# Talking-heads attention and a squared-ReLU network on one core: the first batch's first 22 score chunks taken through four 32-column tiles and one mixing matmul instead of six full matmuls

## The chip, the core and the metric

The kernel runs on one core of one Trainium2 chip. The metric is device time in microseconds, the median of several runs. One more execution was recorded by the hardware profiler; all durations below come from that one. The engines are TensorE (PE in the profile, its weight loads PEld), VectorE (DVE), ScalarE (ACT), GpSimd (POOL) and SyncE (SP).

## The reference, cut to what is computed

```python
# batch 8, 12 heads, 448 positions, head size 64; w_pre and w_post are 12x12
scores = (q @ k^T) / 8                        # per head
scores = einsum('bhij,hg->bgij', scores, w_pre)   # heads mixed before the softmax
attn   = softmax(scores, axis=-1)
attn   = einsum('bhij,hg->bgij', attn, w_post)    # and after it
x      = (attn @ v), heads side by side       # 3584 x 768
out    = relu(x @ w_in)**2 @ w_out            # 768 -> 2048 -> 768
```

## The kernel before, in words

Work is cut by batch. In each batch the 448 query rows are taken in chunks of 10 (`CH`), 45 of them: 10 rows times 12 heads give 120 partitions, so that one matmul with a small constant matrix can mix the heads of a chunk. A unit of work goes through these stages:

- **T** (`emit_T`): q and k of a batch are transposed on TensorE and copied out of PSUM into `qkt` (`tev` tasks). In batch 0 head pairs arrive in three groups `a`, each as a q and a k load.
- **QK** (`emit_QK`): scores of a tile of queries, copied out into `stage` (24 copies of 448 columns for 12 heads of two tiles in batch 0). DMAs from SP (`emit_rel`) move the rows of a chunk from `stage` into a slot of `dring`, which brings all heads of a row together.
- **pre** (`emit_pre`): one 64-wide matmul pair per half chunk mixes the heads with `wk1`. The result is in PSUM.
- **exp** (`after_pre`): ScalarE takes the exponential into `pring` with row sums; `rec` and `fold` put 1/sum into the post-mixing matrix `wk2s` (on VectorE for the first five pairs of chunks, on GpSimd after that).
- **post** (`emit_post`): mixes the heads again and transposes; two copies per pair of chunks into `a2t`.
- **AV**, **F1** (`relu`, `sq`) and **F2** (`oev`, `odma`): attention times v, and the two layers of the network.

Batch 0 has no finished `stage` at the start, so its first 22 chunks (`ND`) take another way in `emit_direct`: VectorE multiplies q with the scaled `w_pre` into `qs` (`emit_scale`, tasks `sc`, which hold 12 mixed copies of each query row), and for each chunk six full 128x128 matmuls, one per head pair, add up the already mixed scores in one PSUM bank (L922). exp reads that bank. `qs` lies in the space of `w_out_sb` (16 chunks) and `h2t` (6 chunks), so `w_out` is loaded after the chunks in its space are done.

TensorE's order is not found at run time: `ORDER` is a string of stream numbers (0 T, 1 QK, 2 pre, 3 post, 4 AV, 5 direct, 6 and 7 F1, 8 and 9 F2), and `_Plan.run` takes the next unit of that stream. The copies out of PSUM are `FLEX` tasks, which the planner gives to ACT or DVE; each engine's list is then fixed. PSUM has 8 banks of 512 columns; a QK or post unit takes two, a chunk of `emit_direct` one. Where the planner sees a gap ahead of a unit in the first 60 us it puts matmuls on constant data there (`warm`).

TensorE works in several tilings, and the planner charges a change of tiling: full 128x128 ("full": direct, F1 of two batches), 64x128 ("row": some QK, post, F1, F2), 64x64 ("quad": T, some QK, pre, F1, F2) and 128x64 ("cols": AV).

## Time and the profile before

| what | us |
|---|---|
| median of 3 runs (lowest, highest) | 519.81 (518.43, 520.98) |
| span of the profiled execution | 520.6 |
| TensorE busy | 505.5 |
| ScalarE busy | 425.6 |
| VectorE busy | 398.7 |
| GpSimd busy | 203.4 |
| first F2 matmul on the chain of work that ended last | 90.46 |

The profiled execution is given by its span, from the first instruction to the last; no separate run time stands beside it, and its span lies 0.8 us above the median of the runs. Matmuls are pipelined: one of 448 columns is shown as about 354 ns, while a row of them starts every 190 ns or so. So TensorE's cost is read from the chain of work (start, length, how many), not from the mean of one matmul. "Busy" of an engine in a stretch counts overlapping instructions once, and the sum of ACT and DVE over twice the stretch says how dense the two engines that empty PSUM are.

### The profile page before, as it was taken

The page shows a single profiled execution, that of the slowest core. Times are in us where ns is not written, and L with a number is a line of the kernel's source. Part 1 is how long each engine was busy: PE and PEld are TensorE (multiplying, and loading weights), DVE is VectorE, ACT ScalarE, POOL GpSimd, SP SyncE. Part 2 cuts the span into 40 slices and gives each one's busy share as a digit, 9 for nine tenths or more (in the row PEclk, how much of TensorE's full clock was granted, in tenths as well). Part 3 has the DMA queues.
Part 4 walks back from the last instruction along what each step waited for, and adds up shares of the span by engine and source line. Part 5 has one row for each costly group of instructions (what it writes and reads, how often), then busy time and mean ns, then how long its engine had stood idle before and what let it go on. Part 6 is the DMA issues. An engine that isn't in the chain of part 4 may idle for free.

```text
span 520.6 us, 25670 instructions
## 1 busy us (share of the span) xinstructions
PE 505.5 (97%) x10859; PEld 340.1 (65%) x10859; DVE 398.7 (77%) x1004; ACT 425.6 (82%) x1206; POOL 203.4 (39%) x404
## 2 busy tenths in 40 slices
PE   8999999899999999999999999999999999999996
PEld 4555777668766665667657665667666666678963
DVE  6967988789987869967997779976887669757430
ACT  4799999879998898989887999988788879878311
POOL 9914364325632384134622464225440333123010
PEclk9999999999999999999999999999999999999999
DMA  8999999646893699347974689457972568432013
GB/s 160 208 218 184 197 194 184 156 107 144 167 180 86 136 177 197 92 112 166 178 156 90 153 175 179 98 111 170 167 151 59 125 140 148 91 81 69 4 39 90
DMA packets 82724, 72.12 MB, mean 139 GB/s; under 512 B 13578, under 2 KB 80090, under 8 KB 82602
## 3 DMA queue, kind: packets, MB, share of 16 engines
q0 software_dynamic: 36944, 32.81, 38.5%
q1 hardware_dynamic: 45370, 37.38, 29.7%
q8 instruction: 89, 1.46, 1.1%
q14 instruction: 33, 0.27, 0.1%
q10 hardware_dynamic: 288, 0.20, 0.1%
HBM read 45.70 MB, written 11.01 MB: 109 GB/s over the span
## 4 chain that ended last, share of the span: by engine, by line
PE 92%; DMA 3%; DVE 2%; issue 2%; ACT 1%; POOL 0%; DVEq 0%
PE ps L1413 17%; PE ps L1278 12%; PE ps L1427 9%; PE ps L1292 9%; PE ps L1133 8%; PE ps L1052 8%; PE ps L1257 6%; PE ps L1211 6%; PE ps L922 5%; PE ps L974 4%; DMA dring<-stage 3%; PE ps L825 2%; PE ps L1362 2%; PE ps L986 2%; PE ps L649 1%
## 5 line engine op out<-in xcount | busy, mean ns | idle before, releaser
L1070 ACT ACTIVATE pring<-ps 128x448 bf16<-128x448 f32 x360 | 192.0, 550 | 12.6 <-PE ps L1052 7.3
L1101 POOL TENSOR_TENSOR wk2s<-wk2b,rinv 128x120 bf16<-128x120 bf16 (+1 forms) x179 | 69.0, 389 | 223.5 <-DVE rinv L1094 222.8
L527 DVE CAST a2t<-ps 128x480 bf16<-128x480 f32 (+1 forms) x201 | 122.1, 640 | 18.4 <-PE ps L1133 16.9
L527 DVE CAST stage<-ps 128x448 bf16<-128x448 f32 (+1 forms) x189 | 112.8, 618 | 19.0 <-PE ps L986 8.7
L526 ACT ACTIVATE stage<-ps 128x448 bf16<-128x448 f32 (+1 forms) x171 | 87.9, 549 | 18.2 <-PE ps L986 10.6
L526 ACT ACTIVATE a2t<-ps 128x480 bf16<-128x480 f32 x167 | 88.2, 570 | 15.5 <-PE ps L1133 15.0
L1413 PE MATMUL ps<-w_out_sb,h2t 64*128 64x384 bf16 x1056 | 95.9, 322 | 0.0
L1070 ACT ACTIVATION_READ_ACCUMULATOR pring<-ps 128x1 f32 x360 | 76.9, 214 | 0.0
L1133 PEld LDWEIGHTS ps<-wk2s,pring 60*128 60x128 bf16 x2880 | 54.9, 93 | 24.7 <-issue 5.8
L1278 PE MATMUL ps<-xt,w_in_sb 64*128 64x448 bf16 (+2 forms) x840 | 70.6, 309 | 0.0
L1413 PEld LDWEIGHTS ps<-w_out_sb,h2t 64*128 64x128 bf16 x1056 | 48.4, 94 | 31.1 <-PE ps L1052 0.7
L1459 POOL DMA_DIRECT2D out_dram<-osb x59 | 36.9, 632 | 75.9 <-DVE osb L527 25.8
L1133 PE MATMUL ps<-wk2s,pring 60*128 60x60 bf16 x2880 | 62.3, 187 | 1.9 <-issue 1.4
L1052 PE MATMUL ps<-dring,wk 64*64 64x448 bf16 (+1 forms) x676 | 61.5, 359 | 2.4 <-issue 1.2
L1427 PE MATMUL ps<-w_out_sb,h2t 64*64 64x384 bf16 x1216 | 57.4, 323 | 0.9 <-issue 0.8
L1323 DVE TENSOR_SCALAR h1t<-ps 128x448 bf16<-128x448 f32 (+2 forms) x96 | 46.2, 488 | 12.6 <-PE ps L1278 9.1
L1292 PE MATMUL ps<-xt,w_in_sb 64*64 64x448 bf16 (+1 forms) x1008 | 54.5, 345 | 0.8 <-issue 0.6
L1332 DVE TENSOR_TENSOR h2t<-h1t 128x448 bf16<-128x448 bf16 (+2 forms) x176 | 52.0, 331 | 1.4 <-ACT h1t L1322 0.9
L1322 ACT ACTIVATE h1t<-ps 128x448 bf16<-128x448 f32 (+2 forms) x80 | 35.4, 448 | 19.7 <-PE ps L1278 13.9
L1094 DVE RECIPROCAL rinv<-rowsum 128x2 f32<-128x2 f32 (+1 forms) x184 | 29.3, 160 | 28.2 <-ACT pring L1070 27.1
L1278 PEld LDWEIGHTS ps<-xt,w_in_sb 64*128 64x128 bf16 x840 | 38.3, 94 | 18.1 <-DVE rinv L1094 0.5
L1427 PEld LDWEIGHTS ps<-w_out_sb,h2t 64*64 64x64 bf16 x1216 | 38.2, 107 | 13.8 <-issue 2.0
(70 smaller groups left out, 595.0 us busy)
## 6 DMA issues: line engine op xcount, KB each, us to landing
dring<-stage SPq DMA_DIRECT2D x309, 105.0 KB
out_dram<-osb POOLq DMA_DIRECT2D x45, 192.0 KB, 3.7
qraw<-in_q_dram POOLq DMA_DIRECT2D x42, 112.0 KB, 5.3
kraw<-in_k_dram POOLq DMA_DIRECT2D x42, 112.0 KB, 6.2
w_in_sb<-in_moe_w_in_dram POOLq DMA_DIRECT2D x8, 384.0 KB, 16.3
w_out_sb<-in_moe_w_out_dram POOLq DMA_DIRECT2D x8, 384.0 KB, 11.9
vraw<-in_v_dram POOLq DMA_DIRECT2D x21, 128.0 KB, 4.8
vraw<-in_v_dram POOLq DMA_DIRECT2D x21, 96.0 KB, 5.0
```

Source lines behind the costliest of these rows:

```text
L526: return eng.activation(o, i_, AF.Copy)
L527: return eng.tensor_copy(o, i_)
L1052: r_ = eng.matmul(ps[64 * y:64 * y + 64, gr.banks[x], 0:S], wk1[64 * x:64 * x + 64 - R0 * x, :], dring[64 * x:64 * x + 64 - R0 * x, (g0 + ...
L1070: return eng.activation(pring[:, pr, 0:S], ps[:, gr.banks[x], 0:S], AF.Exp, accum_out=rowsum[:, rs, :])
L1101: return eng.tensor_tensor(wk2s[:, p0:p0 + n, :], i0.to_broadcast([128, n, PR]), rinv[:, p0:p0 + n, :].to_broadcast([128, n, PR]), ALU.mult)
L1133: r_ = eng.matmul(ps[:, gr.banks[x], o0:o0 + PR], pring[64 * x:64 * x + PR, pr + y, j0:j0 + 2 * PJ], wk2s[64 * x:64 * x + PR, pr + y, :], ...
L1278: r_ = eng.matmul(ps[:, g.banks[x], 0:n], w_in_sb[64 * y:64 * y + 64, ft, t * 128:(t + 1) * 128], xt[64 * y:64 * y + 64, ft, c0:c1], start ...
L1292: r_ = eng.matmul(ps[64 * z:64 * z + 64, g.banks[x], 0:n], w_in_sb[64 * y:64 * y + 64, ft, t:t + 64], xt[64 * y:64 * y + 64, ft, c0:c1], s ...
L1323: return eng.tensor_scalar(h1t[:, box[0], 0:n], ps[:, g.banks[x], 0:n], 0.0, None, op0=ALU.max)
L1332: return eng.tensor_tensor(h2t[:, t16, o0:o0 + n], h1t[:, box[0], 0:n], h1t[:, box[0], 0:n], ALU.mult)
L1413: r_ = eng.matmul(ps[:, g.banks[hh], 0:FH], h2t[64 * y:64 * y + 64, t16, col:col + 128], w_out_sb[64 * y:64 * y + 64, t16, hh * FH:(hh + 1 ...
L1427: r_ = eng.matmul(ps[64 * z:64 * z + 64, g.banks[hh], 0:FH], h2t[64 * y:64 * y + 64, t16, col + 64 * z:col + 64 * z + 64], w_out_sb[64 * y ...
```

## The change

For each of the 22 chunks the scores of the 12 heads are now first computed unmixed, 10 rows of each head, and laid out on 120 of 128 partitions, then mixed by one matmul. The stationary operand for that is `qs[rows, chunk, j, part, 0:32]`, zero but for the columns that belong to one head, so that a matmul of 128 rows (two heads) and 32 columns puts two or one heads' rows in their places. Four such tiles `j` lie side by side in the 128 columns of TensorE, and two matmuls per tile (`part` 0 and 1) add up: 8 matmuls per chunk. Then VectorE or ScalarE copies the 448 columns into a ring of 8 slots (`sring`, task `sv`), and one full matmul with `wks` (scaled `w_pre` with a mask) gives the mixed scores.

- Gone: 132 full matmuls (L922), 36 VectorE multiplications `sc` (L900), four small ones for `wq` (L613), six of the twelve copies of q and k of batch 0 into `qkt` (for q), the load `wall`.
- New: 176 matmuls of 32 columns (L932 of the kernel after), 22 full matmuls `mx` (L949), 22 copies `sv` of 448 columns (14 on ACT and 8 on DVE), 12 copies of 64x220 into `qs` (10 on DVE, 2 on ACT), three copies of the rest of q for QK (128x2x228), a zero fill of `qs` of 2816 32-bit columns on ACT instead of one of 768 and one of 288, a sum for a mask and two products for `wks`, and eight small loads of `w_pre` on SP instead of one. The matmuls of a chunk need all six head pairs of q and k; before, two pairs were enough to begin.
- `w_out` is loaded after all 22 chunks, not after 16. `ORDER` and the unit sizes in `EVENTS` are new throughout, so all units of the kernel stand in a new order. Matmuls of other kinds are the same in number; three more `warm` matmuls stand in it (20 for 17).
- Counted along TensorE's order, the tiling changes 252 times before and 267 times now; ahead of the first F2 matmul 82 and 116 times, and after it 170 and 151 times. Up to that matmul both orders hold the same units, but for one pre unit (90 matmuls before, 86 now) and two QK units in another tiling.

The core of the diff (`ORDER` is left out but for a line):

```diff
-    "0001501510105151555555555555555551335510015555555553335510021551355553255310055511255321"
+    "00101001101155555a15aa5155a555aa30aa3011a55aa1a53351553aaa555a0a33aa5a0a2a33323001144114"
...
+        def fn_wreps(eng, en):
+            for j in range(TL):
+                for c, n, h in ((0, 2, head(j, 0)), (2, 1, head(TL + j // 2, j % 2))):
+                    src = bass.AP(w_pre.tensor, h * H, [[2 * H, n], [0, CH], [1, H]])
+                    r0 = 32 * j + c * CH
+                    eng.dma_start(wreps[r0:r0 + n * CH, :], src).then_inc(sem_ws.handle, 16)
...
-                            emit_scale(p)
+                                for x in range(2):
+                                    rows = slice(64 * x, 64 * x + 64)
+                                    j, part, o0 = (p, 0, x * CH) if p < TL else (
+                                        2 * (p - TL) + x, 1, 2 * CH)
+                                    r_ = copy(eng, en, qs[rows, :, j, part, o0:o0 + CH],
+                                              ps_bf[rows, g.banks[0], u * S:u * S + ND * CH].rearrange(
+                                                  "p (c a) -> p c a", a=CH))
...
-                for p in ps_:
-                    r_ = eng.matmul(ps[:, g.banks[0], 0:S],
-                                    qs[:, p, y:y + 2, :].rearrange("p i g -> p (i g)"),
-                                    qkt[:, 0, p, 1, :],
...
+                for part in range(2):
+                    for j in range(TL):
+                        p = TL + j // 2 if part else j
+                        r_ = eng.matmul(ps[32 * j:32 * j + 32, g.banks[0], 0:S],
+                                        qs[:, c, j, part, :], qkt[:, 0, p, 1, :],
+                                        start=(part == 0), stop=(part == 1))
...
+            t_sv = add("sv%d" % c, FLEX, fn_sv, [t, dir_done.get(c - NSR)], c_ev(S), -500.0 + c)
+            g.readers[0].append(t_sv)
+            g2 = _Group(1)
+
+            def fn_mx(eng, en):
+                return eng.matmul(ps[:, g2.banks[0], 0:S], wks[:, :], sring[:, slot, :],
+                                  start=True, stop=True)
...
-                emit_load_w(1, [dir_done[c] for c in range(NDW)])
+                emit_load_w(1, [dir_done[c] for c in range(ND)])
```

Three places show how it moves instructions. The first is TensorE from the last transpose of batch 0 on. Before, the six-matmul chunks are L922 (`ps<-qkt,w_out_sb`), QK is L974 and L986, post is L1133:

```order
L821 MATMUL ps<-ident,kraw 64x2x32 x28
L922 MATMUL ps<-qkt,w_out_sb 128x448 x2
L974 MATMUL ps<-qkt 128x448 x2
L922 MATMUL ps<-qkt,w_out_sb 128x448 x2
L974 MATMUL ps<-qkt 128x448 x2
L922 MATMUL ps<-qkt,w_out_sb 128x448 x37
L974 MATMUL ps<-qkt 128x448 x2
L1133 MATMUL ps<-wk2s,pring 128x60 x32
```

Now the narrow matmuls are L932, the mixing matmul is L949 (`ps<-w_out_sb,osb`: `sring` and `wks`), and QK is L990:

```order
L851 MATMUL ps<-ident,kraw 64x2x32 x28
L665 MATMUL ps<-warm 128x448 x3
L990 MATMUL ps<-qkt 128x448 x4
L932 MATMUL ps<-qkt,w_out_sb 32x448 x40
L949 MATMUL ps<-w_out_sb,osb 128x448
L990 MATMUL ps<-qkt 128x448 x2
L932 MATMUL ps<-qkt,w_out_sb 32x448 x8
L949 MATMUL ps<-w_out_sb,osb 128x448 x2
L932 MATMUL ps<-qkt,w_out_sb 32x448 x8
L990 MATMUL ps<-qkt 128x448 x2
```

Where 37 matmuls of one tiling stood in a row, narrow groups, mixing matmuls and QK units now alternate, and all of the chunks' matmuls stand behind the last transpose (four stood ahead of it).

The second place is VectorE at the same time. Before, the copies of q and k (`qkt<-ps`) are followed by the scaled copies L900 (`w_out_sb<-qkt,osb`):

```order
L527 CAST qraw<-xt 128x896
L527 COPY qkt<-ps 128x448
L562 TENSOR_TENSOR mask<-mask 128x5
L527 COPY qkt<-ps 128x448
L613 TENSOR_SCALAR osb<-osb 64x180 x4
L900 TENSOR_TENSOR w_out_sb<-qkt,osb 128x8x60 x2
```

Now the copies go straight into `qs` (`w_out_sb<-ps`), and L630, which needs the eight small loads of `w_pre`, stands ahead of the copies of the second and third head groups:

```order
L531 CAST qraw<-xt 128x896
L531 COPY w_out_sb<-ps 64x22x10 x2
L568 TENSOR_TENSOR mask<-mask 128x5
L531 COPY w_out_sb<-ps 64x22x10 x2
L531 COPY qkt<-ps 128x2x228
L531 COPY qkt<-ps 128x448
L630 SCALAR_TENSOR_TENSOR osb<-osb 128x60 x2
L531 CAST stage<-ps 128x448
L531 COPY w_out_sb<-ps 64x22x10 x2
```

What moved is a wait: VectorE now reaches a product that needs small DMAs before it has copied out the later groups.

The third place is ScalarE where its exponentials begin (`pring,rowsum<-ps`). Before:

```order
L526 ACTIVATE stage<-ps 128x448 x9
L1070 ACTIVATE pring,rowsum<-ps 128x448 x7
L526 ACTIVATE stage<-ps 128x448
L526 ACTIVATE a2t<-ps 128x48x2x5 x2
L1070 ACTIVATE pring,rowsum<-ps 128x448
```

Now, with the copies `sv` as `w_out_sb<-ps 128x448`:

```order
L530 ACTIVATE stage<-ps 128x448 x5
L530 ACTIVATE w_out_sb<-ps 128x448 x4
L1086 ACTIVATE pring,rowsum<-ps 128x448
L530 ACTIVATE stage<-ps 128x448
L1086 ACTIVATE pring,rowsum<-ps 128x448 x2
L530 ACTIVATE stage<-ps 128x448
L530 ACTIVATE w_out_sb<-ps 128x448 x2
L1086 ACTIVATE pring,rowsum<-ps 128x448
```

The copies `sv` stand in among the exponentials, and each chunk's exponential now has a copy and a second matmul ahead of it.

More of the change, by code (lines that the diff above doesn't have):

```diff
@@ L522, in unit, with head @@
             return t
+        def head(p, c):
+            return 4 * (p % 3) + 2 * c + p // 3
         def copy(eng, en, o, i_):
@@ L838, in emit_T @@
                         continue
+                    last = None
                     for u in range(2):
                         p = 3 * u + a
-                        def fn_ev(eng, en, u=u, p=p, g=g, i=i):
-                            return copy(eng, en, qkt[:, 0, p, i, :],
-                                        ps_bf[:, g.banks[0], u * S:(u + 1) * S])
-                        t_ev = add("tev0_%d_%d" % (p, i), FLEX, fn_ev, [t_tr, trev.get((0, p - 3, i))],
-                                   {ACT: (447.0, 597.0), DVE: (309.0, 400.0)}, -4e5)
@@ new lines, in emit_T, with fn_ev @@
+                        g.readers[0].append(last)
+                        trev[(0, p, i)] = last
+                        if i:
+                            trev[(0, p)] = last
+                    if i == 0:
+                        def fn_ev(eng, en, a=a, g=g):
+                            return copy(eng, en, qkt[:, 0, a:NP:3, 0, Q0:S],
+                                        ps_bf[:, g.banks[0], 0:2 * S].rearrange(
+                                            "p (u k) -> p u k", u=2)[:, :, Q0:S])
+                        last = add("tev0_%d_r" % a, FLEX, fn_ev, [t_tr, last],
+                                   {ACT: (2 * (S - Q0) / 1.2 + 75.0, 2 * (S - Q0) / 1.2 + 225.0),
+                                    DVE: (2 * (S - Q0) / 1.92 + 75.0, 2 * (S - Q0) / 1.92 + 165.0)}, -3e5)
+                        g.readers[0].append(last)
+                        rest_of[a] = last
```

181 lines of the change are left out of this document (78 added, 103 removed).

## Prediction

> **What bounds the kernel now.** I read the page first, then the busy time by stretches, then the chain of work that ended last, then the groups of instructions by line and shape. The first line of the page's list of engines:
>
> ```profile
> PE 505.5 (97%) x10859; PEld 340.1 (65%) x10859; DVE 398.7 (77%) x1004; ACT 425.6 (82%) x1206; POOL 203.4 (39%) x404
> ```
>
> TensorE is busy for 97% of the span. The change acts on the first batch, so the stretches matter more; they are cut at 90.46 us, where the first F2 matmul starts on the chain:
>
> ```profile
> core 0: us, PE busy (x) PEld busy (x) DVE busy (x) ACT busy (x) POOL busy (x), PEclk, DMA share, GB/s
> 10.00:90.46 80.46, 78.03 (x1416) 50.45 (x1420) 67.49 (x198) 73.46 (x215) 40.65 (x76) 1.00 1.12 198
> 60.00:70.00 10.00, 9.75 (x168) 7.50 (x166) 9.30 (x29) 9.70 (x29) 4.55 (x9) 1.00 1.05 190
> 90.46:500.00 409.54, 403.84 (x9221) 276.83 (x9214) 324.37 (x783) 346.58 (x984) 151.41 (x305) 1.00 0.63 130
> ```
>
> From 10 to 90.46 us TensorE is busy for 78.03 of 80.46 us, but ScalarE and VectorE together work 73.46 + 67.49 = 140.95 of 160.92 us, or 87.6%. The densest ten us quoted hold 9.30 + 9.70 = 19.0 of 20, or 95%. So the start is TensorE's, with the two engines that empty PSUM close behind. After 90.46 us TensorE has 98.6% and the other two 82%: there a saving on TensorE would show in full. The chain in the early stretch, and one later AV unit, price the steps (start, length, what):
>
> ```profile
> 15.04 7.10 PE ps L922 x37
> 30.40 0.77 PE ps L1133 x48
> 32.41 0.31 PE ps L986 x4
> 33.20 0.26 PE ps L1052 x4
> 33.46 0.19 PE ps L986 x4
> 35.19 0.22 PE ps L1133 x16
> 57.10 2.37 PE ps L1257 x24
> 90.46 1.34 PE ps L1427 x32
> 100.32 1.25 PE ps L1211 x24
> ```
>
> **TensorE, part by part.** A full matmul of 448 columns takes 7.10/37 = 0.192 us, so the 132 that go away take 25.3 us.
>
> The 22 mixing matmuls come at the same price: 22 x 0.192 = 4.2 us.
>
> The 128x32 tiles are not in this trace. The nearest rows are other tilings. Four 64x64 matmuls of 448 columns with no change of tiling ahead take 0.19 us (33.46), so four tiles do run at once there. In the AV unit 24 matmuls of 128x64 take 1.25 us, 104 ns for a pair, while full matmuls of the same 220 columns take 2.37/24 = 99 ns: two tiles of 128 rows also run at once, at no loss. From these I take 0.19 us for four narrow tiles, 0.38 us for a chunk's eight, 22 x 0.38 = 8.4 us in all. The upper bound is a row of full matmuls, as if no two tiles overlapped: 8 x 0.192 = 1.54 us per chunk. Below 0.38 us I see no reason to go, since 448 columns have to be streamed twice.
>
> A change of tiling: L986 takes 0.31 us behind a full matmul and 0.19 us without a change; L1133 takes 0.22 us per 16 without, and 0.77 us per 48 with one, 0.11 us more. I take 0.11 us. Up to the first F2 matmul there are 116 - 82 = 34 more, +3.7 us; after it 170 - 151 = 19 fewer, -2.1 us. The three extra warm matmuls fill gaps and cost nothing.
>
> TensorE's sum up to the first F2 matmul is -25.3 + 4.2 + 8.4 + 3.7 = -9.0 us, after it -2.1 us. If nothing else were in the way, the first F2 matmul would start at 90.46 - 9.0 = 81.5 us.
>
> **ScalarE and VectorE, part by part.** The groups by shape that answer to what goes and comes (count | busy in all, mean ns of one), and between them ScalarE's first copy in order of time:
>
> ```profile
> L900 DVE TENSOR_TENSOR w_out_sb<-qkt,osb 128x480 bf16<-128x480 bf16 x24 | 9.4, 448 | 0.1
> L900 DVE TENSOR_TENSOR h2t<-qkt,osb 128x480 bf16<-128x480 bf16 x6 | 2.6, 450 | 0.0
> L900 DVE TENSOR_TENSOR h2t<-qkt,osb 128x240 bf16<-128x240 bf16 x6 | 1.4, 304 | 0.0
> L613 DVE TENSOR_SCALAR osb<-osb 64x180 bf16<-64x180 f32 x4 | 1.2, 328 | 0.0
> L527 DVE COPY qkt<-ps 128x448 bf16<-128x448 bf16 x11 | 3.9, 383 | 1.2 <-PE ps L821 1.2
> L527 DVE CAST stage<-ps 128x448 bf16<-128x448 f32 x147 | 86.8, 617 | 16.9 <-PE ps L986 8.7 <-PE ps L974 6.8 <-DMA dring<-stage 0.9
> L526 ACT ACTIVATE stage<-ps 128x448 bf16<-128x448 f32 x129 | 65.5, 553 | 16.8 <-PE ps L986 10.6 <-PE ps L974 5.9 <-PE ps L1052 0.2
> 9.86 0.98 ACT L526 ACTIVATE stage<-ps 128x448 bf16<-128x448 f32 x2 [6.59 <-PE ps L986]
> L882 ACT ACTIVATE w_out_sb<-wk 128x768 bf16<-128x768 bf16 x1 | 0.8, 843 | 0.0
> L882 ACT ACTIVATE h2t<-wk 128x288 bf16<-128x288 bf16 x1 | 0.4, 427 | 0.0
> L623 DVE SCALAR_TENSOR_TENSOR wk<-wrep,mask 128x60 bf16<-128x60 f32 x1 | 0.2, 206 | 0.0
> ```
>
> Gone are 9.4 + 2.6 + 1.4 + 1.2 = 14.6 us on VectorE, and six copies of q at 3.9/11 = 0.35 us, 2.1 us: 16.7 us. New are the copies `sv`, whose nearest row is `stage`: 8 x 86.8/147 + 14 x 65.5/129 = 4.7 + 7.1 = 11.8 us. The 12 copies into `qs` have 220 columns, a shape not in the trace; half a 448-column copy (0.18 us) and a whole one (0.35 us) bound them, and I take 0.25 us: 3.0 us. Three copies of the rest of q: 1.1 us. Products and mask: 0.6 us. That is 16.5 us, as much as goes. The zero fill grows: 843 - 427 ns for 480 columns more is 0.87 ns a column, so 2816 columns take about 2.6 us instead of 1.3 us; ScalarE has nothing else before 9.86 us in this trace, which hides it, and uncovered it would cost 1.3 us.
>
> Up to the first F2 matmul the two engines therefore still have about 141 us of work after the first 10 us, 70.5 us each. This is where TensorE's saving is stopped: at 100% the landmark is at 80.5 us, at the 95% of the densest quoted stretch at 84.2 us, at today's 87.6% at 90.5 us. I choose 92%: the engines wait less, since TensorE is ahead of them, but each of the 22 chunks now also has a chain of narrow matmuls, copy, mixing matmul, exponential, and PSUM banks are held twice. That gives 10 + 70.5/0.92 = 86.6 us, 3.9 us earlier, which is later than TensorE's 81.5 us.
>
> **Queues and waits.** SP issues eight small loads of `w_pre` where it issued one, ahead of the zero DMA and the other small weights. Rows of SP's queue, of VectorE's list, and of the DMA issues:
>
> ```profile
> 0.81 0.41 SPq L698 DMA_DIRECT2D xt<-in_q_dram  x1
> 1.27 0.42 SPq L602 DMA_DIRECT2D osb<-in_w_pre_dram  x1
> 7.19 0.88 SPq L594 DMA_DIRECT2D wrep<-in_w_pre_dram  x1
> 16.18 53.78 SPq L1029 DMA_DIRECT2D dring<-stage  x40
> 1.51 0.11 DVE L541 MEMSET ident<- 128x64 uint32 x1
> 6.30 0.39 DVE L527 COPY qkt<-ps 128x448 bf16<-128x448 bf16 x1 [1.25 <-PE ps L821]
> osb<-in_w_pre_dram SPq DMA_DIRECT2D x1, 72.0 KB, 5.1
> xt<-in_q_dram SPq DMA_DIRECT2D x1, 448.0 KB, 3.6
> ```
>
> They wait for the initial fills (1.6 us), so eight issues of 0.42 to 0.88 us end at 5.0 to 8.7 us, and the last, landing 3.6 to 5.1 us later, is there at 8.6 to 13.8 us. VectorE reaches the product that needs them some 1.8 us of copies (four into `qs`, the rest of q, one of k) after 6.30 us, at about 8.1 us. It stands still there for 0.5 to 5.7 us, and behind it wait the copies of the second and third head groups, then all narrow matmuls. I take the middle, 3 us; ScalarE works on, so half of that, 1.5 us, is in the 92%. The worst end puts 2.8 - 1.5 = 1.3 us more on the result; the best end, 0.2 us, takes as much off. The zero DMA, the small weights and SP's moves stand behind the loads too, but the moves begin at 16.18 us and the first pre unit that needs them is at 33.20 us, so I cost that at nothing.
>
> `w_out` now waits for all 22 chunks. Its last piece was issued here, and its pieces landed in:
>
> ```profile
> 62.83 0.79 POOL L753 DMA_DIRECT2D w_out_sb<-in_moe_w_out_dram  x1
> w_out_sb<-in_moe_w_out_dram POOLq DMA_DIRECT2D x8, 384.0 KB, 11.9
> ```
>
> So it was there at about 74.7 us, 15.7 us ahead of its first use; POOL's list keeps about as many folds ahead of it, and I cost it at nothing. If that cover went, F2 would wait for the difference.
>
> **The sum.** The span after the landmark is 520.6 - 90.46 = 430.1 us, less 2.1 us: 428.0 us. 86.6 + 428.0 = 514.6 us against 520.6. The median of the runs is 0.8 us below the profiled span, so I forecast 513.8 us. With 89% to 95% for the two engines the landmark is at 89.2 to 84.2 us, the time 511.4 to 516.4 us; with both ends of the small loads 510 to 518 us.
>
> The Trainium skill, TensorEngine Tiling (Array Packing), section Performance Considerations, says that tiling speeds TensorE up and not the emptying of PSUM, which may then become the bound. The 87.6% above agrees that this is near; it is the first rival.
>
> **Rivals.**
> *No denser than now (0.21).* The two engines stay at 87.6%, waiting on the longer chain of each chunk, and the landmark stays at 90.5 us. Only the fewer changes of tiling later remain: 90.5 + 428.0 - 0.8 = 517.7 us. For it: 14 of the copies `sv` stand among the exponentials, which only ScalarE can do, and a chunk takes one of 8 banks of PSUM twice. Against it: 95% is reached from 60 to 70 us.
>
> *All of TensorE's saving (0.08).* The landmark is at 81.5 us, the time 508.7 us. For it: TensorE is busy for 78.03 of the 80.46 us now. Against it: the other two would have to work 70.5 of 71.5 us.
>
> *The narrow tiles don't overlap (0.10).* Four tiles of 128 rows read four sets of 128 rows at once, which no row here shows. At 1.54 us per chunk TensorE has 22 x (1.54 - 0.38) = 25.5 us more, the landmark is at 81.5 + 25.5 = 107.0 us, and the time 107.0 + 428.0 - 0.8 = 534.2 us, slower than before. It decides from 0.38 + 11.1/22 = 0.88 us per chunk; two tiles at a time (0.77 us) would still not be slower. Against it: the AV and 64x64 rows.
>
> *Their weight loads wait (0.06).* This row gives a load in the AV tiling:
>
> ```profile
> L1211 PEld LDWEIGHTS ps<-a2t,vraw 128*64 128x64 bf16 x640 | 29.6, 109 | 5.4 <-issue 4.5 <-DVE rinv L1094 0.3 <-ACT stage L526 0.2
> ```
>
> If each of a chunk's eight loads of 109 ns held up the matmuls, TensorE would have 22 x 0.87 = 19.2 us more, the landmark at 100.7 us and the time at 527.9 us; it decides from 0.50 us per chunk. Against it: those 24 AV matmuls with their loads take 1.25 us in all, and loads that waited would alone take 2.6 us. The Trainium skill, TensorE: Matmul & The Clock Gate, section Part 3: Packing small matmuls, says that weight loads overlap with matmuls in flight only where the row group differs, which here it never does. The AV row disagrees for two tiles; for four, no run here shows it.
>
> **How the numbers follow.** The forecast has 0.55. A measurement of this kernel can tell about 0.5%, 2.6 us, so "same" is 517.2 to 522.4 us. Faster: 0.52 of the forecast, 0.08, and 0.06 of the first rival, 0.66. Same: 0.03 and 0.15, 0.18. Slower: the last two, 0.16. The range leaves out the last two and little else: 507 to 522 us.
>
> **What would show it.** Right: eight narrow matmuls in about 0.38 us on the chain; ScalarE and VectorE at about 92% from 10 us to the first F2 matmul, which starts near 86.6 us; about 428 us from there on; VectorE idle ahead of the products for `wks`. Wrong: a chunk above 0.5 us on TensorE, a landmark at 90 us or later, a later stretch that isn't shorter, or F2 waiting for `w_out`.

## The result and the profile after

The kernel after takes 526.32 us (median, 519.68 to 533.64) against 519.81 us: slower, ratio 1.0093 with a 95% interval of 1.0064 to 1.0121. Forecast were 513.8 us and a range of 507 to 522 us. The profiled execution of the kernel after took 528.71 us with a span of 527.0 us, 2.4 us above the median. Medians below are over all executions, while the ratios leave out those far above the fastest, so that the two can differ (e2, e12); the profiled execution of the kernel after is one of the slower ones.

The page's list of engines, after:

```profile
PE 500.8 (95%) x10908; PEld 333.8 (63%) x10908; DVE 397.0 (75%) x992; ACT 424.7 (81%) x1213; POOL 204.2 (39%) x404
```

TensorE has 4.7 us less work than before and a span 6.4 us longer, so the loss is waiting. The stretches of the kernel after, cut at its own first F2 matmul (93.37 us) and with the ten us at the start taken apart:

```profile
10.00:20.00 10.00, 4.87 (x94) 2.48 (x87) 5.21 (x17) 2.84 (x8) 10.00 (x19) 0.66 1.36 198
10.00:93.37 83.37, 74.30 (x1467) 44.98 (x1462) 66.53 (x184) 73.45 (x219) 40.28 (x75) 0.94 1.07 189
93.37:527.00 433.63, 418.71 (x9330) 284.74 (x9326) 326.06 (x788) 345.93 (x991) 155.12 (x310) 1.00 0.61 127
```

The first ten us and the later stretch of the kernel before, for comparison:

```profile
10.00:20.00 10.00, 9.83 (x135) 4.96 (x136) 9.96 (x31) 6.82 (x17) 10.00 (x18) 1.00 1.35 200
90.46:520.60 430.14, 419.41 (x9345) 285.82 (x9336) 325.48 (x785) 349.53 (x990) 153.93 (x309) 1.00 0.62 127
```

Two losses, then. The first F2 matmul comes 2.9 us later instead of 3.9 us earlier, and from there on it takes 433.6 us instead of 430.1 (428.0 were forecast). From 10 to 20 us TensorE worked for 4.87 us instead of 9.83, at a granted clock of 0.66. The timeline shows why (start, length, engine, what, and in brackets the idle time ahead of it and what ended it):

```profile
1.75 6.72 SPq L611 DMA_DIRECT2D osb<-in_w_pre_dram  x8
13.73 0.35 DVE L630 SCALAR_TENSOR_TENSOR osb<-osb 128x60 bf16<-128x60 f32 x2 [5.36 <-DMA osb<-in_w_pre_dram]
16.39 0.96 PE L1002 MATMUL ps<-qkt 64*64 64x448 bf16 x8 [4.98 <-DVE qkt L531]
```

SP needs 6.72 us to issue the eight small loads of `w_pre`; the last lands at 13.7 us, VectorE stands for 5.36 us ahead of the product `wks`, and behind it wait the copies without which TensorE has nothing. The chain of waits of the kernel after, four places in the order of time:

```profile
7.74 5.97 DMA osb<-in_w_pre_dram
...
20.09 2.00 PE ps L932 x40
...
25.61 1.25 PE ps L932 x24
...
80.41 11.98 DMA kraw<-in_k_dram
...
93.37 1.32 PE ps L1429 x16
```

The narrow matmuls are as cheap as forecast: 40 in 2.00 us, 0.40 us per chunk of eight. The last stretch ahead of the first F2 matmul is a load of `k` for a later batch, which took 11.98 us. TensorE had other work meanwhile; its transposes stood for the load for the last 0.92 us.

What TensorE waited for, after:

```profile
PE ps L1002 <- DVE qkt L531: 5.4, 2, 5.0
PE ps L855 <- issue: 3.7, 4, 1.4
PE ps L1149 <- issue: 2.9, 3, 1.4
PE ps L1308 <- issue: 1.8, 1, 1.8
PE ps L1068 <- issue: 1.7, 1, 1.7
```

And before, where the largest of these stops was 1.0 us:

```profile
PE ps L825 <- issue: 1.8, 2, 1.0
PE ps L1133 <- issue: 1.4, 3, 0.6
PE ps L1052 <- issue: 1.2, 2, 1.0
```

"issue" is time in which TensorE waits for nothing that the profile shows. The prediction had not asked about these stops. They have one thing in common: when TensorE's instructions are counted along the program (a matmul is two, its weight load and itself, and a wait that stands alone is one), all 20 of them, in both kernels, fall at the same place in a row of 256, that is, at the end of each block of 256 instructions. I take a stop to be what a step between two matmuls has over the usual step between two of the same shapes, within two matmuls of such a place. The sum is 13.4 us before (1.2 us of it ahead of the first F2) and 19.8 us after (3.1 us of it).

### The profile page after: what moved, and what is told of

Read it like the earlier page. It is cut to its first block, busy times and chain, and to the rows that moved or that the text cites. A ratio compares the mean times of both kernels' runs of the same rounds, so it can differ in the third digit from the quotient of the medians.

```text
span 527.0 us, 25754 instructions
## 1 busy us (share of the span) xinstructions
PE 500.8 (95%) x10908; PEld 333.8 (63%) x10908; DVE 397.0 (75%) x992; ACT 424.7 (81%) x1213; POOL 204.2 (39%) x404
## 4 chain that ended last, share of the span: by engine, by line
PE 83%; DMA 4%; DVE 4%; issue 3%; ACT 3%; POOL 2%; SPq 1%
PE ps L1429 16%; PE ps L1294 12%; PE ps L1443 9%; PE ps L1149 8%; PE ps L1308 7%; PE ps L1068 7%; PE ps L1227 6%; PE ps L1273 5%; PE ps L990 4%; DMA kraw<-in_k_dram 2%; PE ps L1378 2%; PE ps L1002 2%; PE ps L855 2%; PE ps L932 2%; ACT pring L1086 2%
## 5 line engine op out<-in xcount | busy, mean ns | idle before, releaser
L1086 ACT ACTIVATE pring<-ps 128x448 bf16<-128x448 f32 x360 | 192.1, 553 | 17.6 <-PE ps L1068 14.9
L531 DVE CAST stage<-ps 128x448 bf16<-128x448 f32 (+1 forms) x201 | 119.6, 618 | 18.2 <-PE ps L1002 6.8
L531 DVE CAST a2t<-ps 128x480 bf16<-128x480 f32 (+1 forms) x196 | 118.3, 637 | 18.4 <-PE ps L1149 17.6
L530 ACT ACTIVATE a2t<-ps 128x480 bf16<-128x480 f32 (+1 forms) x172 | 91.2, 579 | 15.2 <-PE ps L1149 14.7
L530 ACT ACTIVATE stage<-ps 128x448 bf16<-128x448 f32 (+1 forms) x159 | 82.4, 550 | 17.5 <-PE ps L990 8.4
L1294 PE MATMUL ps<-xt,w_in_sb 64*128 64x448 bf16 (+2 forms) x876 | 74.2, 309 | 0.2 <-DVE a2t L531 0.2
L1068 PE MATMUL ps<-dring,wk 60*64 60x448 bf16 (+1 forms) x676 | 60.5, 359 | 1.9 <-issue 1.7
L1339 DVE TENSOR_SCALAR h1t<-ps 128x448 bf16<-128x448 f32 (+2 forms) x87 | 42.5, 493 | 17.1 <-PE ps L1294 11.4
L1294 PEld LDWEIGHTS ps<-xt,w_in_sb 64*128 64x128 bf16 x876 | 40.5, 94 | 20.4 <-ACT pring L1086 0.7
L1338 ACT ACTIVATE h1t<-ps 128x448 bf16<-128x448 f32 (+2 forms) x89 | 39.3, 453 | 16.5 <-PE ps L1294 14.5
L1308 PE MATMUL ps<-xt,w_in_sb 64*64 64x448 bf16 (+1 forms) x936 | 50.5, 347 | 1.9 <-issue 1.8
```

The costliest lines, as they stand in the source:

```text
L530: return eng.activation(o, i_, AF.Copy)
L531: return eng.tensor_copy(o, i_)
L1068: r_ = eng.matmul(ps[64 * y:64 * y + 64, gr.banks[x], 0:S], wk1[64 * x:64 * x + 64 - R0 * x, :], dring[64 * x:64 * x + 64 - R0 * x, (g0 + ...
L1086: return eng.activation(pring[:, pr, 0:S], ps[:, gr.banks[x], 0:S], AF.Exp, accum_out=rowsum[:, rs, :])
L1294: r_ = eng.matmul(ps[:, g.banks[x], 0:n], w_in_sb[64 * y:64 * y + 64, ft, t * 128:(t + 1) * 128], xt[64 * y:64 * y + 64, ft, c0:c1], start ...
L1308: r_ = eng.matmul(ps[64 * z:64 * z + 64, g.banks[x], 0:n], w_in_sb[64 * y:64 * y + 64, ft, t:t + 64], xt[64 * y:64 * y + 64, ft, c0:c1], s ...
```

## The experiments

The theories: the start is held up by the small loads (undo that, and the start comes forward by about as much as VectorE stood); the later loss comes from the stops at the ends of blocks, either because the units stand in another order (L) or because the ends fall in other places (P). All runs in a table, so that the text can be short. "First F2" is the start of the first matmul of F2 in its record (the chain shows it 0.16 us later), "rest" the time from there to the end of the last matmul, "stops" their sum ahead of and behind the first F2, as above; these three are of one execution each.

| run | median us | ratio to before (95%) | first F2 | rest | stops |
|---|---|---|---|---|---|
| before | 519.81 | | 90.3 | 425.3 | 1.2, 12.2 |
| after | 526.32 | 1.0093 (1.0064 to 1.0121) | 93.2 | 428.8 | 3.1, 16.7 |
| e1 after, `wks` late | 526.57 | 1.0083 (1.0041 to 1.0126) | 89.2 | 431.5 | 5.4, 15.8 |
| e2 after, padded to the planner's count | 532.37 | 1.0102 (1.0025 to 1.0180) | 94.4 | 433.2 | 4.8, 15.3 |
| e3 both | 529.44 | 1.0188 (1.0146 to 1.0229) | 93.5 | 429.4 | 6.9, 12.6 |
| e4 before, eight loads | 526.17 | 1.0122 (1.0079 to 1.0166) | 95.9 | 424.1 | 1.7, 10.2 |
| e5 new start, old later order | 532.17 | 1.0251 (1.0195 to 1.0307) | 94.9 | 425.4 | 2.9, 11.8 |
| e6 the same, block ends as before | 529.56 | 1.0167 (1.0111 to 1.0223) | 98.4 | 424.0 | 4.7, 7.9 |
| e7 old start, new later order | 523.60 | 1.0108 (1.0054 to 1.0161) | 90.3 | 426.5 | 1.7, 9.6 |
| e8 before, 127 waits in the start | 527.64 | 1.0157 (1.0112 to 1.0201) | 91.1 | 427.9 | 2.2, 14.2 |
| e9 before, 255 waits in the start | 528.28 | 1.0133 (1.0077 to 1.0188) | 99.7 | 424.0 | 3.3, 8.2 |
| e10 e1 with 64 waits | 527.73 | 1.0139 (1.0092 to 1.0186) | 91.5 | 431.9 | 6.3, 16.0 |
| e11 e1 with 128 waits | 527.69 | 1.0144 (1.0091 to 1.0197) | 93.6 | 423.5 | 6.4, 9.7 |
| e12 e1 with 192 waits | 532.52 | 1.0150 (1.0058 to 1.0241) | 94.9 | 427.2 | 7.4, 12.1 |
| e13 e1, half the narrow matmuls | 525.71 | 1.0106 (1.0067 to 1.0145) | 89.2 | 430.1 | 2.3, 12.1 |
| e14 e1, half the copies | 525.84 | 1.0103 (1.0050 to 1.0156) | 89.8 | 430.2 | 4.8, 14.8 |
| e15 before, 128 waits later | 532.80 | 1.0260 (1.0221 to 1.0298) | 90.0 | 437.5 | 1.4, 17.6 |
| e16 after, 128 waits later | 529.48 | 1.0165 (1.0115 to 1.0215) | 93.1 | 429.8 | 3.4, 8.3 |
| e17 before, 256 waits later | 531.95 | 1.0194 (1.0155 to 1.0234) | 91.2 | 437.5 | 0.4, 11.7 |
| e18 e1, half of both | 526.07 | 1.0135 (1.0083 to 1.0187) | 89.8 | 429.6 | 4.3, 13.1 |

None of them is faster than the kernel before.

### The small loads: e1 and e4

In e1 the product that needs the loads moves behind the copies, directly ahead of the first mixing matmul:

```diff
         per_engine, committed = plan.run(ORDER)
+        committed.remove(t_wks)
+        first_mx = next(i for i, t in enumerate(committed) if t.name == "mx0")
+        committed.insert(first_mx, t_wks)
```

> The kernel after, with the two products for wks moved on VectorE's list from ahead of the second head group's copies to just ahead of the first mixing matmul's own inputs; all else stands in the same order. Theory A (the eight small loads stop VectorE, everything behind it waits and TensorE's clock falls): VectorE's 5.4 us of idle time ahead of the products goes, the first narrow matmul starts near 15 us instead of 20.09, at most 2 us of it lost again to the other small weights that SP issues behind the loads; no stretch with a clock below 1.00 from 10 to 20 us; first F2 matmul near 88 us instead of 93.4; time 5 us below the kernel after (ratio to before 1.000). Rival B (the copies out of PSUM bound the start anyway): the narrow matmuls start earlier but the first F2 matmul stays within 1.5 us of 93.4, ratio to before 1.007 or more.

The first narrow matmuls and the wait behind them, in e1's timeline:

```profile
14.15 2.15 PE L932 MATMUL ps<-qkt,w_out_sb 128*32 128x448 bf16 x40
17.66 0.35 PE L949 MATMUL ps<-w_out_sb,osb 128*128 128x448 bf16 x1 [1.35 <-DVE osb L630]
```

They start at 14.15 us instead of 20.02, and the first F2 matmul at 89.2 instead of 93.2 us: the wait costs the kernel after 4.0 us there. In e4 the kernel before gets the same eight issues for its one load of `w_pre` (16 partitions each):

```diff
-            src = bass.AP(w_pre.tensor, 0, [[0, 128], [1, H * H]])
-            eng.dma_start(wall[:, :, :, :].rearrange("p a b c -> p (a b c)"), src).then_inc(
-                sem_wq.handle, 16)
+            for r0 in range(0, 128, 16):
+                src = bass.AP(w_pre.tensor, 0, [[0, 16], [1, H * H]])
+                eng.dma_start(wall[r0:r0 + 16, :, :, :].rearrange("p a b c -> p (a b c)"),
+                              src).then_inc(sem_wq.handle, 16)
...
-        t_wall = plan.add("wall", SP, fn_wall, [], {SP: (400.0, 5300.0)}, -1e6 - 1, sem_wq, 16)
+        t_wall = plan.add("wall", SP, fn_wall, [], {SP: (400.0, 5300.0)}, -1e6 - 1, sem_wq, 128)
```

> The kernel before, with its one load of w_pre for the products wq cut into eight loads of 16 partitions on SP; nothing else changes. Theory A: VectorE waits 5 to 6 us for the last of them ahead of wq, TensorE's first full stream of narrow-chunk matmuls starts that much later, with a low clock on some of it: 5 to 7 us slower, ratio 1.010 to 1.013. Rival B: the start has slack, under 1.5 us, ratio below 1.003.

VectorE and TensorE stand in e4's timeline as they do in the kernel after:

```profile
11.63 1.20 DVE L614 TENSOR_SCALAR osb<-osb 64x180 bf16<-64x180 f32 x4 [4.51 <-DMA osb<-in_w_pre_dram]
14.02 0.59 PE L987 MATMUL ps<-qkt 64*64 64x448 bf16 x4 [4.78 <-DVE qkt L527]
```

First F2 5.6 us later, median 6.2 us above the 520.0 us that the kernel before took beside it, ratio 1.0122. So eight small issues ahead of something that VectorE waits for cost the kernel before about as much as the whole change costs (6.2 us against 6.5, ratios 1.0122 and 1.0093). That is shown, and so, in one execution each, are the 4.0 us at the first F2 matmul. Yet e1 as a whole is no faster than the kernel after: 526.57 us. Its span is only 1.1 us shorter, and the trace gives back more than half of the 4.0 us at one place, a stop at a block's end that the kernel after has too (1.40 us there):

```profile
381.01 0.25 PE L855 MATMUL ps<-ident,kraw 64*64 64x64 bf16 x6 [1.96 <-issue]
```

and, in e1's stretches of two us from 380 on, a clock of about half behind it:

```profile
380.00:382.00 2.00, 0.99 (x26) 0.81 (x30) 0.69 (x2) 0.51 (x2) 0.00 (x0) 1.00 0.48 76
382.00:384.00 2.00, 2.00 (x32) 1.37 (x28) 1.48 (x4) 1.30 (x7) 0.97 (x2) 0.54 0.59 120
384.00:386.00 2.00, 2.00 (x32) 1.39 (x28) 1.13 (x5) 0.68 (x4) 0.82 (x2) 0.60 0.83 125
```

A clock of 0.54 and 0.60 for two us each is 0.92 + 0.80 = 1.7 us of lost work. Whether the other executions of e1 lose the lead in the same place no trace shows; the medians say that it is lost. So the wait is shown as the cause of the late start, not of the longer time as a whole.

### What else holds the start: e13, e14, e18

Without the wait the first F2 matmul is at 89.2 us, and the two engines that empty PSUM work at the density of the kernel before. e1, 10 us to its first F2:

```profile
10.00:89.35 79.35, 71.48 (x1445) 43.55 (x1446) 65.57 (x181) 73.45 (x219) 40.09 (x74) 1.00 1.11 196
```

That is (73.45 + 65.57) / 158.7 = 87.6%. e13 takes work from TensorE (the last two head pairs are left out of the first 22 chunks), e14 from the two others (the second half of these chunks' scores is left out), e18 does both:

```diff
-                for part in range(2):
+                for part in range(1):
...
-                                        start=(part == 0), stop=(part == 1))
+                                        start=True, stop=True)
```

```diff
-                return copy(eng, en, sring[:, slot, :], ps[:, g.banks[0], 0:S])
+                return copy(eng, en, sring[:, slot, 0:S // 2], ps[:, g.banks[0], 0:S // 2])
...
+                half = sring[:, slot, 0:S // 2].unsqueeze(1).to_broadcast([128, 2, S // 2])
-                return eng.matmul(ps[:, g2.banks[0], 0:S], wks[:, :], sring[:, slot, :],
+                return eng.matmul(ps[:, g2.banks[0], 0:S], wks[:, :], half,
```

> The kernel after with the product for wks moved behind the copies, and only the first four of each chunk's eight narrow matmuls (the heads of the last two pairs are left out of the scores of these chunks): 88 matmuls, 176 instructions and about 4.4 us less on TensorE, all else as it was. Theory T (the start is TensorE's own time and its stops): first F2 at 84 to 85 us instead of 89.2 us. Theory E (ScalarE and VectorE hold it): first F2 within 1 us of 89.2 us.

> The kernel after with the product for wks moved behind the copies, and copies sv of 224 columns instead of 448; the mixing matmul reads these 224 columns twice (the second half of the scores of these chunks is left out), so TensorE's work stays. 14 x 0.25 us less on ScalarE and 8 x 0.3 us less on VectorE, 5.9 us in all or about 3 us for each. Theory T: first F2 within 1 us of 89.2 us. Theory E: first F2 at 85.5 to 87 us.

> The kernel after with the product for wks moved behind the copies, with four narrow matmuls per chunk instead of eight and copies sv of 224 columns (the last two head pairs and the second half of the scores of these chunks are left out). Theory J (TensorE and the engines that empty PSUM hold the start about equally, so that relief of one alone shows nothing): first F2 3 to 4 us earlier than 89.2 us. Rival X (something else holds it, the moves of SP or the exponentials behind 50 us): first F2 within 1 us of 89.2 us.

None of the three moves the first F2 matmul: 89.2, 89.8 and 89.8 us. The numbers of T (e13), E (e14) and J (e18) did not come, and X's is left. The chain of waits shows something that X had not named, a load. It is this stretch in e1:

```profile
76.51 11.86 DMA kraw<-in_k_dram
```

the same stretch of the chain in e13:

```profile
76.19 12.20 DMA kraw<-in_k_dram
```

and in e18:

```profile
74.68 13.79 DMA kraw<-in_k_dram
```

The load of `k` ends at 88.37, 88.39 and 88.47 us (88.92 in e14), though it was issued between 74.7 and 77.4 us, and the transposes that need it are on TensorE directly ahead of the first F2 unit. In e1 TensorE stood for it for 0.80 us:

```profile
88.42 0.41 PE L855 MATMUL ps<-ident,kraw 64*64 64x64 bf16 x28 [0.80 <-DMA kraw<-in_k_dram]
```

and longest in e18, where all else was earlier:

```profile
88.52 0.59 PE L855 MATMUL ps<-ident,kraw 64*64 64x64 bf16 x28 [2.73 <-DMA kraw<-in_k_dram]
```

POOL issues these loads behind six loads of `v` (3.7 us of issue), and those behind the pieces of `w_out`, of which six are issued between 54.66 and 67.1 us in the kernel after, and two from 55 us on (60.19, 62.83) in the kernel before. The DMA engines are busy at that time (share 1.11 from 70 to 80 us in e1), and such a load takes twelve us where the page's median is 5.5.

So the load is a floor that hid what e18 had gained: its TensorE came to the transposes 1.8 us earlier than that of e1, about half of what J had forecast. Another part was lost ahead of that, for at the first mixing matmul TensorE waited longer for `wks` (2.8 us in e13 and 2.3 in e18 against 1.35 in e1). But the load is not all that holds the start. Without it e1's first F2 matmul could come only 0.80 us earlier. The rest is open: e1 has 5.4 us of stops ahead of that matmul where the kernel before has 1.2, and its ScalarE is busy for 9.9 us or more of each ten from 50 to 80 us. Whether it is the later `w_out` that makes the load late was not tried.

### Order and places of the block ends: e2, e3, e5 to e7

The planner prices the stops by its own count of TensorE's instructions (`fetch_wait`), and the order was probably written with these prices. For the new units the count is one too high (`sx` and `mx`: 1.0 in `EVENTS`, an instruction that the program does not have), and at the end of the kernel after it is 88 ahead. e2 adds 146 waits that are long fulfilled (88 instructions in the trace; here and below two waits of the program can make one instruction, and the numbers in the table count instructions), spread so that the program's count follows the planner's; e3 does that to e1.

```diff
             for t, fn, ws in what:
+                n_pad = PADS.count(t.name) if e == PE else 0
+                for _ in range(n_pad + (1 if n_pad and not ws else 0)):
+                    eng.wait_ge(ctr[DVE].handle, 1)
                 for s_, v_ in ws:
```

> The kernel after, with some 90 waits that are already fulfilled put between TensorE's units, so that the count of its instructions follows the count that the planner worked with (it counted one extra instruction for each narrow and each mixing unit, which the program does not have, and is 88 ahead at the end). Theory C (TensorE stops at every 256th of its instructions when the next block has not come, and the new order was laid for other block ends): the idle time of TensorE put down to issue falls from 10.7 us to about 6 us, most of it after 93 us, and the time falls by 3 to 5 us (ratio to before 1.000 to 1.003). Rival D (these stops go with the DMA traffic or are chance, wherever the block ends lie): no change beyond 1.5 us, ratio 1.007 to 1.012.

> Both edits on the kernel after. A and C both right: the gains add, 8 to 10 us below the kernel after, ratio to before 0.990 to 0.994, faster than before. B and D: ratio 1.005 or more. If A alone holds: about 1.000.

Ratios of 1.0102 and 1.0188, where C had forecast 1.003 and 0.994 at most, and stops of 20.1 and 19.5 us: no cure. e2's interval just reaches C's number, e3's does not. The count was not it.

e5 and e6 put the old order of the later units behind the new start, e7 the new one behind the old start. The streams' counts agree at the 143rd unit of the one and the 149th of the other, so that the strings can be cut there:

```diff
-ORDER = (after)
+ORDER = after[:143] + before[149:]     # e5, e6; e7: before[:149] + after[143:]
```

> The narrow chunks and the new order up to the 143rd unit (about 68 us), from there the order of the kernel before (its units from the 149th on; the counts per stream agree at this point, so nothing is left out or done twice). Theory L (the new order of the later units is itself worse by the 3.5 us that its later stretch is longer): first F2 near 93.4 us, 430 us from there on, median about 522.8 us. Theory P (what costs is where the ends of the blocks of 256 TensorE instructions fall; the order before has them in better places): this kernel has 129 to 138 more TensorE instructions ahead of the old units than before, half a block, so the ends fall elsewhere; stops stay near 18 to 20 us in sum, median 525 to 528 us.

> As the run before, with waits that are long fulfilled added to TensorE's list between about 10 and 40 us until the old units stand 254 to 262 instructions behind their old place, so that every block of 256 ends within 6 instructions of where it ended before. Theory L: the same as without these waits, about 522.8 us. Theory P: stops fall back to about 13 to 15 us in sum, median about 522 to 523 us and 3 to 5 us below the run without them.

> The kernel before with its six-matmul chunks and its order up to the 149th unit, from there the new order (after's units from the 143rd on). Theory L: first F2 near 90.5 us, 433.6 us from there on, median about 523.3 us. Theory P: the ends of the blocks fall half a block away from where they fall in the kernel after, and the time is not fixed by the order alone: 519 to 527 us with stops of 13 to 20 us in sum.

e7 is slower without a single narrow matmul: by its ratio as much as the whole change (1.0108 against 1.0093), by its median half as much (3.4 us above the kernel before beside it, against 6.5), and its profiled execution is 1.2 us longer than before behind the first F2, not 3.5. But e5 and e6 do not win it back, as both theories had said that one of them would. Their rest is short (425.4 and 424.0 us, as in the kernel before), their start is worse (94.9 and 98.4 us), and their granted clock over the executions is 0.981 to 0.990 where the kernel before beside them had 0.997 to 1.000. L's number for e7 (523.3 us) was met; for e5 (522.8 us) it was missed by 9 us, P's (525 to 528 us) by 4; e5's six executions lie between 525.6 and 535.4 us. A start and a later order that each do well with another partner do badly together: the pieces do not add up.

### Moving the block ends alone: e8 to e12, e15 to e17

If places matter and not the order, then waits that do nothing must change the time by moving the ends, and a whole block's worth of them must not. e8 and e9 put them into the start, at some 64 units of the kernel before.

> The kernel before, all units in the same order and on the same engines, with 127 instructions more on TensorE (waits that are long fulfilled, four at each of 63 units between about 12 and 60 us), so that all later blocks of 256 end half a block earlier. Theory L (and that the waits cost nothing): 519.8 us, same as before. Theory P: stops of 17 to 22 us in sum instead of 13.4, 3 to 8 us slower, about 525 us.

> The kernel before with 255 fulfilled waits more on TensorE (eight at each of about 64 units), twice as many as in the run with 127, so that all later blocks of 256 end one instruction from where they ended before. Theory P (the places of the block ends cost): 519 to 522 us, as before, stops of 12 to 15 us in sum. Rival W (the added waits themselves cost, 7.4 us for 127 of them): about 535 us.

e8 loses 7.4 us, as P had it, but e9 loses 7.9 us (the kernel before beside it took 520.4 us), which fits neither P (519 to 522 us) nor W (535 us). The trace takes e9's loss apart: it is 9.4 us late at the first F2 matmul, so eight waits at a unit are not free in the start, and 1.2 us faster than before from there on, with 8.2 us of stops. e8 is 0.8 us late there and 2.6 us slower after it, with 14.2 us of stops. W holds in the start and P behind it, in one execution each.

e10 to e12 did the same to e1.

> The kernel after with the product for wks moved behind the copies, and 64 fulfilled waits on TensorE between about 10 and 45 us, so that later blocks of 256 end a quarter of a block earlier; same units in the same order on the same engines. Theory P: anywhere from 519 to 530 us, and different from the unshifted kernel's 526.6 by several us in one of the three shifted runs at least. Theory L (the order of units alone sets the time): 526.6 us within 1.5 us in all three.

> The same with 128 waits, half a block. Theory P: 519 to 530 us, not the same in all three shifted runs. Theory L: 526.6 us within 1.5 us.

> The same with 192 waits, three quarters of a block. Theory P: 519 to 530 us, not the same in all three shifted runs. Theory L: 526.6 us within 1.5 us.

527.73, 527.69 and 532.52 us, each with a later first F2 (91.5 to 94.9 us). That is not the same in all three, as P said, but what the waits cost in the start hides the rest in the medians. In the traces it can be seen apart: behind the first F2 e11, half a block off, takes 423.5 us with 9.7 us of stops, where e1 takes 431.5 us with 15.8. But e11's profiled execution is the fastest of its six, 3.5 us below their median. So e15, e16 and e17 put them at 32 units of F2 and F1 between about 91 and 195 us, the last two to tell 128 from 256:

> The kernel before with 128 fulfilled waits on TensorE, four at each of 32 units of F2 and F1 between about 91 and 190 us, none in the start; from about 193 us on every block of 256 ends half a block earlier. Theory P (places of the block ends): stops after the first F2 of 14 us and more instead of 12.2, and 2 to 5 us slower, 522 to 525 us. Theory L (the order itself): 520 us, the same as before.

> The kernel after with 128 fulfilled waits in the same way, at 32 units of F2 and F1 between about 94 and 195 us. Theory P (its places are unlucky): stops after the first F2 fall from 16.7 to 10 to 13 us, 3 to 5 us faster than the kernel after, 521 to 523 us. Theory L: 526.3 us within 1.5 us.

> The kernel before with 256 fulfilled waits at the same 32 units of F2 and F1 (eight at each instead of four), so that from about 193 us on every block of 256 ends exactly where it ended before. Theory P (the places of the block ends): from 195 us to the end as in the kernel before, stops there of 4 to 7 us in sum; what the waits cost between 91 and 195 us, about 3 us with 128 of them, may double: 521 to 526 us, well below the 532.8 us with half as many waits. Rival W (the waits themselves cost): 545 us or more.

Neither P's nor W's number came for e17. To see the two costs apart, one pre unit near 200 us and the last F2 unit of the chain are compared, first in the kernel before. The timeline's row of the pre unit:

```profile
198.70 0.39 PE L1052 MATMUL ps<-dring,wk 64*64 64x448 bf16 x4
```

and the chain's of the last F2 unit:

```profile
505.07 10.52 PE ps L1362 x64
```

Then e15's timeline, with the post unit that follows that pre unit:

```profile
202.16 0.39 PE L1052 MATMUL ps<-dring,wk 64*64 64x448 bf16 x4
...
205.88 0.32 PE L1133 MATMUL ps<-wk2s,pring 60*128 60x60 bf16 x11 [3.14 <-issue]
```

and its chain:

```profile
517.07 10.52 PE ps L1362 x64
```

And e17, timeline and chain:

```profile
209.06 0.39 PE L1052 MATMUL ps<-dring,wk 64*64 64x448 bf16 x4
```

Its last F2 unit:

```profile
518.22 10.52 PE ps L1362 x64
```

At the pre unit e15 is 202.16 - 198.70 = 3.5 us late and e17 10.4 us: with twice the waits the cost grew from about 29 to about 37 ns each, stops on the way included, where TensorE is never idle. From there to the last F2 unit e15 loses another 12.0 - 3.5 = 8.5 us, 3.1 us of it in the one stop above, and e17, whose blocks end where those of before end, 13.15 - 10.36 = 2.8 us. So half a block's shift with all units in place costs some 6 us more than a whole block's, in one execution each, and the medians keep e15 (128 waits) above e17 (256).

e5 with e6 and e8 with e9 are two more such pairs, since the later units of e5 stand 129 instructions behind their place in the kernel before and those of e6 254: half a block has 11.8, 14.2 and 17.6 us of stops behind the first F2 (e5, e8, e15), a whole block 7.9, 8.2 and 11.7 (e6, e9, e17). The kernel before in its own places has 12.2, so single executions differ by some 4 us at the same places.

The new order shows it the other way round. In its own places it has 16.7, 15.8 and 14.8 us of stops (after, e1, e14), half a block off 9.6, 9.7 and 8.3 (e7, e11, e16; e7 has 131 instructions less ahead than the kernel after). So the stops go with the places, and the order before stands well where the new one stands badly. That much of P is shown, over twelve traces. That the places make the change's loss in time is not: behind the first F2 the new order takes 428.8, 431.5 and 430.2 us in its own places and 426.5, 423.5 and 429.8 us half a block off, but the medians don't follow, and profiled executions lie up to 6.6 us (e5) from their medians. e16's stops fell by half, and yet it is 3.2 us slower than the kernel after. About 2.5 us went to the waits by 190 us, and ahead of 267.4 us ScalarE and VectorE stood for 3.4 and 3.5 us for the moves of SP.

## Why the prediction was wrong, point by point

For the profiled span the sum gave 514.6 us, and 527.0 were measured. Of the 12.4 us between them 6.8 lie ahead of the first F2 matmul and 5.6 behind it.

- **The narrow matmuls** (0.38 us per chunk): right, 0.40 to 0.42 us. The two rivals that priced them higher fall (the 0.50 us from which the second decides is meant on top of the 0.38). Their weight loads, by the group below, take 8 x 95 ns = 0.76 us per chunk by themselves, so they ran beside the matmuls; the Trainium skill, TensorE: Matmul & The Clock Gate, section Part 3: Packing small matmuls, says that they overlap only where the row group differs, and this trace disagrees for four tiles of 32 columns too (40 matmuls in 2.00 us).

The groups of the kernel after that answer to the copies and fills (count | busy, mean ns of one):

```profile
L932 PEld LDWEIGHTS ps<-qkt,w_out_sb 128*32 128x32 bf16 x176 | 3.7, 95 | 5.2 <-issue 2.2 <-ACT w_out_sb L530 0.6 <-ACT stage L530 0.4
L530 ACT ACTIVATE w_out_sb<-ps 128x448 bf16<-128x448 f32 x14 | 7.1, 591 | 0.0
L531 DVE CAST w_out_sb<-ps 128x448 bf16<-128x448 f32 x8 | 4.9, 622 | 1.7 <-PE ps L932 1.7
L531 DVE COPY w_out_sb<-ps 64x220 bf16<-64x220 bf16 x10 | 2.7, 268 | 1.6 <-PE ps L851 1.5
L826 ACT ACTIVATE w_out_sb<-osb 128x2816 f32<-128x2816 f32 x1 | 2.6, 2551 | 0.3 <-DVE osb L591 0.3
```

- **The copies' and fills' sizes**: right. `sv` took 7.1 + 4.9 us (forecast 7.1 + 4.7), one copy into `qs` 268 ns (250), the fill 2.55 us (2.6). ScalarE and VectorE together had 73.45 + 66.53 = 140.0 us up to the first F2, forecast were 141.
- **The small loads**: the mechanism was right, the size was not. The range of 0.5 to 5.7 us held the 5.36 us, the middle (3 us) was the wrong choice, and the step "ScalarE works on, so half of that" was wrong: TensorE stood for 4.98 us, and the first F2 matmul moved by 4.0 us where 1.5 was counted. That is 2.5 us of the 6.8 by which the landmark was missed (93.4 instead of 86.6 us).
- **The density of 92%**: wrong, and for a reason that the prediction did not have. e1, without the wait, is at 87.6%, the number of the rival "No denser than now". That rival's reason, the longer chain of each chunk, is neither shown nor excluded, since in e14 and e18 the load of `k` hid what a shorter chain would bring. The failed step is that TensorE's saving was to be stopped by ScalarE and VectorE alone. Two other things stood in its way: the stops at block ends ahead of the first F2 (3.1 us in the kernel after and 5.4 in e1, against 1.2 before), and the load of `k` on POOL's queue (0.92 and 0.80 us). The prediction looked at SP's queue and asked of POOL's only whether F2 would wait for `w_out`; it did not ask what else POOL issues there and who waits for it. The other 4.3 us of the landmark stand in e1 as well, 89.35 on the chain where the prediction has 85.1 without its 1.5 us for the small loads. The two causes come to 5.0 us there, if every one of them reached the landmark, which no run shows; how these 4.3 us divide stays open.
- **`w_out` at no cost**: F2 did not wait for it, as forecast. Six of its eight pieces now go out from 54.66 us on, ahead of the loads just named; what that costs stays open.
- **The later stretch, 428.0 us**: wrong, 433.6 us. Fewer changes of tiling may be worth their 2.1 us; they cannot be seen, since the stops at block ends grew from 12.2 to 16.7 us. The prediction read the stretch as "a saving on TensorE would show in full" and left out that any new order, and any instruction added ahead of it, moves all later block ends. The runs show that this alone is worth several us (e15 against e17). How much of the 3.5 us is the order and how much the places is not settled. The traces speak for the places: half a block off, the new order takes 426.5 and 423.5 us behind the first F2 (e7, e11), near the 425.3 of the kernel before. The medians of e5, e6, e11 and e16 speak against either alone.
- **The sign.** No rival had the right cause; slower had been given a chance only by narrow tiles that would not overlap.

## What to carry to other kernels

Before a load is cut into several small ones, find the first instruction that waits for the last of them, and count everything that stands behind that instruction in its engine's list; each issue costs its place in a queue. In a kernel whose tightest engine is busy for 97% of the time, ask what that engine's saving would meet next on every queue, that of the loads for the next stage included. And where an order has been laid out to the instruction, a change of a few instructions early on can move the time later by more than the edit is worth: measure the edit with the rest held still, and expect that pieces do not add up.

## What the runs showed of the hardware

- **Stops at every 256th instruction.** Over all 20 traces and behind the first F2, the stop at a block's end against the time in which TensorE ran through the block ahead of it: under 4 us, 126 blocks, 0.6 to 1.0 us in the mean and up to 3.3; 4 to 5 us, 0.27 us; 5 to 6 us, 0.18; 6 to 8 us, 0.08; over 8 us, 0.03. In the start they are longer: some 0.7 us in the mean for blocks of 5 to 6 us. Half a block's shift changes which blocks are that short: of blocks that took about 3.5 us or less the kernel before has one, e17 one, e15 seven. Short blocks alone do not make a slow run: e5 has seven too, and 11.8 us of stops. The page counts 89 packets of the queue for instructions in either kernel; why a stop is 3.1 us in one run and nothing in another at nearly the same place no view shows.
- **The clock falls to half for 3.4 us or 6.8 us, behind some stops and not behind others.** In all 20 traces the granted clock is 1.00 or 0.50, and each fall but the one at the very end lasts one of these two times. Up to its last matmuls the kernel before has none, the kernel after has two (6.8 us from 13.0 us on, 3.4 us from 47.2), and e1 one (3.4 us from 382.2). It is not the profiled execution alone: over its executions the kernel after had a mean clock of 0.983 to 0.996, the kernel before beside e1 0.993 to 1.000. What these falls are worth in time was not tried. The kernel after from 46 us on, behind 1.65 us of idle TensorE in the eight us from 40 to 48:

```profile
46.00:48.00 2.00, 1.47 (x65) 1.18 (x65) 1.91 (x5) 1.54 (x5) 0.81 (x2) 0.79 0.86 190
48.00:50.00 2.00, 2.00 (x23) 1.04 (x16) 0.85 (x2) 1.38 (x4) 0.32 (x1) 0.50 1.13 173
50.00:52.00 2.00, 2.00 (x30) 1.03 (x28) 1.29 (x4) 1.78 (x4) 0.00 (x0) 0.85 1.14 207
```

The same kernel kept a clock of 1.00 from 260 to 266 us although TensorE was idle for 1.84 of the first four us there.
- **A wait that is fulfilled is not free.** On TensorE it cost about 29 to 37 ns, stops on the way included, where the engine was never idle (e15, e17), and 255 instructions of them at 64 units of the start made it 9.4 us later (e9); at most units of e2 those added left the step to the next matmul the same to 1 ns.
